# Scaled keys split over VectorE and ScalarE, and half of wo times the gradient on VectorE, in a decode layer's forward and backward pass

## The chip, the cores and the metric

The kernel runs on one core of a Trainium2 chip. A core has TensorE (matmuls, written PE in the profile; PEld is its weight loads), VectorE (DVE), ScalarE (ACT), GpSimd (POOL) and SyncE (SP), and 16 DMA engines that move data between HBM and the on-chip memory SBUF. Matmul results land in PSUM and are copied to SBUF by VectorE or ScalarE. Each engine runs its own instructions in order; between engines there are semaphores. The order of instructions on each engine and the waits are laid down by a scheduler when the kernel is built.

The metric is the device time of the kernel in microseconds (us), the median of several runs. Verdicts are taken at 2%.

## What is computed

One decoding step (one new token for each of two sequences) of a transformer layer, and its gradients. Attention reads the last W = 4096 of 32768 cached positions; 32 query heads share 8 heads of keys and values. Cut to what matters:

```python
def _A_ref(x, k_cache, v_cache, wq, wo):          # attention; Hq=32, Hkv=8, Dh=128, W=4096
    q = (x @ wq) ...                              # heads of the one new token
    k = k_cache[:, :, Sk - W:, :] ; v = v_cache[:, :, Sk - W:, :]   # each used by 4 query heads
    p = softmax(q . k * Dh ** -0.5)
    o = p . v
    return o.reshape(B, 1, Hq * Dh) @ wo
def _B_ref(x, w_gate, w_up, w_down):              # feed-forward, F=1792
    return (gelu(x @ w_gate) * (x @ w_up)) @ w_down
h  = x + _A_ref(layernorm(x), k_cache, v_cache, wq, wo)
h2 = h + _B_ref(layernorm(h), w_gate, w_up, w_down)
# outputs: h2, and the gradients for x, k_cache, v_cache, wq, wo, w_gate, w_up, w_down, given grad_out
```

The gradients of the two caches are as large as the caches, 2 x 8 x 32768 x 128 bf16 each, and zero outside the window: 235 MB of zeros are written.

## The kernel before

GpSimd issues 32 writes of zeros at the start, which run beside everything else. Then, for batch 0 and batch 1 in turn: `attention(b)`, `middle(b)` (output projection, feed-forward, and their backward pass down to the gradient of the attention output), `score_grads(b)`; then the weight gradients, and the stores of the gradients of K and V in the window.

Most of SBUF is one tile, `mem`, whose regions are reused by hand. The key buffers K_OFF[1] and the buffers PK_OFF[1] of batch 1 lie on the regions of w_down and of the small rows (OFF_R). `ef` are the exponentials of one group (4 heads, 4096 positions) in float32; `ee` is the same in bf16 with each value stored twice. In `attention`, for each group g and each unit u of 4 key columns:

```python
                KT_ps = ps_KT.tile([P, 8, P], BF16, tag="kt", name="KT_ps")
                for jj in range(8):
                    nc.tensor.transpose(out=KT_ps[:, jj, :], in_=Kt[b, g][:, u * 8 + jj, :], identity=ident_bf[:])
                KT = at(OFF_KT + (u % 2) * 2 * KIB, [P, 8, P], BF16, "KT")
                nc.scalar.copy(out=KT[:], in_=KT_ps[:])
                return KT
# ... (softmax of a group: maximum over all positions, then)
                ef = stA.tile([P, NJ, REP], F32, tag="ef", name="ef", bufs=1)
                ee = stA.tile([P, NJ, REP, 2], BF16, tag="ee", name="ee")
                nc.vector.tensor_tensor(out=ef[:], in0=S[:], in1=negm[:].unsqueeze(1).to_broadcast([P, NJ, REP]), op=ALU.add)
                nc.scalar.activation(out=ef[:], in_=ef[:], func=ACT.Exp)
                nc.vector.tensor_copy(out=ee[:], in_=ef[:].unsqueeze(3).to_broadcast([P, NJ, REP, 2]))
                Ef[g] = ee
                nc.vector.tensor_copy(out=eT[:].rearrange("p j a q -> p a j q")[:, :, :, g * REP:(g + 1) * REP],
                                      in_=ef[:].rearrange("p (a j) i -> p a j i", a=4))
                nc.vector.reduce_sum(out=lsum[:, 0, g * REP:(g + 1) * REP], in_=ef[:].rearrange("p j h -> p h j"), axis=AX.X)

            def m_unit(g, u, M_ps):
                pk = at(PK_OFF[b][u % n_pk], [P, pk_j, REP, DH], BF16, "pK")
                ef, Kb = Ef[g], Kt[b, g]
                j0 = u * pk_j
                shape = [P, pk_j, DH // 2, 2]
                for i in range(REP):
                    nc.vector.tensor_tensor(out=pk[:, :, i, :].rearrange("p j (d t) -> p j d t", t=2),
                                            in0=Kb[:, j0:j0 + pk_j, :].rearrange("p j (d t) -> p j d t", t=2),
                                            in1=ef[:, j0:j0 + pk_j, i, :].unsqueeze(2).to_broadcast(shape), op=ALU.mult)
                for a, src in enumerate((Vt[b, g], Kb)):
                    for jj in range(pk_j):
                        j = j0 + jj
                        c = j % 4
                        nc.tensor.matmul(out=oPK_ps[32 * c:32 * c + REP, a, :], lhsT=eT[:, j % 8, j // 8, g * REP:(g + 1) * REP],
                                         rhs=src[:, j, :], start=(j < 4 and a == 0), stop=(j >= NJ - 4), skip_group_check=True)
                for jj in range(pk_j):
                    j = j0 + jj
                    nc.tensor.matmul(out=M_ps[:], lhsT=Vt[b, g][:, j, :], rhs=pk[:, jj, :, :].rearrange("p i d -> p (i d)"),
                                     start=(j == 0), stop=(j == NJ - 1))

```

M is the sum over positions of v times the scaled keys; it is used later for the gradient of q. `finish(g)` copies oPK_ps and M_ps to SBUF (M on ScalarE). The loop over units makes the transposed keys and the scores of group g + 1 beside the units of group g:

```python
            softmax(0)
            for g in range(HKV):
                if g:
                    prefetch(b, g)
                M_ps = ps_M.tile([P, REP * DH], F32, tag="M", name="M_ps")
                more = g + 1 < HKV
                for u in range(n_u):
                    v, first = u // kt_every, u % kt_every == 0
                    if more and v < 4 and first:
                        nxt = kt_unit(g + 1, v)
                        if v:
                            s_unit(g + 1, v - 1, kts)
                        kts = nxt
                    m_unit(g, u, M_ps)
                    if more and v == 3 and u % kt_every == kt_every - 1:
                        s_unit(g + 1, 3, kts)
                        softmax(g + 1)
                finish(g, M_ps)
```

Loads of keys and values are issued by SyncE as buffers come free (`load_k`, `load_v` in `prefetch`); the values of group g lie at g * 8 KiB. At the end of attention the weights come back, and for batch 1 the two rows:

```python
K_OFF = ([OFF_WG + (g % 4) * 8 * KIB for g in range(HKV)],
         [OFF_WD, OFF_WD + 8 * KIB, 32 * KIB, 40 * KIB, 48 * KIB, 56 * KIB, OFF_WD, OFF_WD + 8 * KIB])
PK_J = 4
PK_OFF = ([OFF_WG + 32 * KIB + i * 4 * KIB for i in range(3)],
          [OFF_WD + 16 * KIB + i * 4 * KIB for i in range(2)])
# ...
    dh2_x = at(OFF_XR, [66, D], BF16, "xr")
    dh2_bf, x_32, dh_bf = dh2_x[0:B, :], dh2_x[32:32 + B, :], dh2_x[64:64 + B, :]

    def load_rows(eng):
        eng.dma_start(out=dh2_bf, in_=grad_out.rearrange("b s d -> (b s) d"))
        eng.dma_start(out=x_32, in_=A_x.rearrange("b s d -> (b s) d"))
# ... in prefetch(b, g), for b == 1:
        else:
            if g == 0:
                for i in range(4):
                    load_k(1, i)
                    load_v(1, i)
                load_k(1, 4)
                load_k(1, 5)
            elif g in (1, 2):
                load_k(1, g + 5)
            elif g - 3 + 4 < HKV:
                load_v(1, g + 1)
# ... for both:
        if g == HKV:
            if b == 0:
                load_wg_wu()
            load_wd()
            if b == 1:
                load_rows(nc.sync)
```

In `middle(b)`, the first matmuls, and the product of wo with the gradient dh, in which every 128 rows of wo are transposed by TensorE in four pieces, copied to SBUF, and multiplied:

```python
            attn_ps = ps_B.tile([B, D], F32)
            nc.tensor.matmul(out=attn_ps[:], lhsT=ident_bf[32:32 + B, 32:32 + B], rhs=x_32, start=True, stop=False)
# ...
            for r in range(NOR):
                nc.tensor.matmul(out=attn_ps[:], lhsT=O2[:, r, :], rhs=wo_sb[:, r, :], start=False, stop=(r == NOR - 1))
# ... feed-forward, forward and backward; for b == 1 ffn_ps with w_down
    def tblock(ps_pool, src_block):
        ps = ps_pool.tile([P, 4, P], BF16, tag="ps_tb", name="ps_tb")
        for a in range(4):
            nc.tensor.transpose(out=ps[:, a, :], in_=src_block(a), identity=ident_bf[:])
        dst = at(OFF_KT + (tb_i[0] % 3) * KIB, [P, 4, P], BF16, "tb")
        tb_i[0] += 1
        evac(dst[:], ps[:])
        return dst
# ...
            ln_bwd(d_ln2_ps[:].rearrange("b a p -> b p a"), ln2[:], rstd2, dh2_bf, f"2{b}", dh, at(OFF_R0, [B, D], F32, "tmp"))
            nc.vector.tensor_copy(out=dh_bf, in_=dh[:])
            dhT = transpose_rows(ps_B.tile([P, NDR, B], BF16, tag="sm", name="psT_dh"), dh_bf, f"dh{b}", strided=False, p0=64)

            dO2_ps = ps_B.tile([P, NOR, B], F32, tag="da", name="dO2_ps")

            def use_woT(r, woT):
                for nt in range(NDR):
                    nc.tensor.matmul(out=dO2_ps[:, r, :], lhsT=woT[:, nt, :], rhs=dhT[:, nt, :], start=(nt == 0), stop=(nt == NDR - 1))
            pipelined(NOR, lambda r: tblock(ps_W, lambda nt: wo_sb[:, r, nt * P:(nt + 1) * P]), use_woT, depth=2)
            # ... dO_sel, which reads dO2_ps[:, :, b]
```

`evac` copies from PSUM on VectorE and ScalarE in turn. `pipelined(n, produce, consume, depth)` runs produce `depth` items ahead.

## Time and profile before

| | |
|---|---|
| time, median of 3 runs | 809.6 us (809.58 to 809.68) |
| span of the profiled run | 807.8 us, mean granted TensorE clock 0.801 |
| busy: PE, PEld, DVE, ACT, POOL | 596.8, 325.7, 463.7, 283.1, 36.5 us |
| moved by DMA | 332.46 MB, mean 412 GB/s |
| of which zeros written by GpSimd's queue | 234.88 MB |

How to read it. A row of the page's groups has the line of the kernel, engine, operation, output and inputs with shapes, the count, then busy time in us and mean ns of one, then the engine's idle time just before and what ended it. The chain follows the work that ended last back to the start; in order of time each row has its start, its length, and what ran or what was waited for. In the page's strip the span is cut into 40 slices of about 20 us; a digit is a busy share in tenths. Where a line number is that of a helper (`evac`, `tblock`), the tile's name tells which use it is: ps_tb are the weight transposes of `middle`, KT_ps the transposed keys, VT_ps the transposed values of `score_grads`.

### The profile page before, as it was taken

The numbers are of one execution on the slowest core, as the hardware profiler recorded it, in microseconds if no ns is written. First come the engines' busy times: TensorE is split into PE (matmuls) and PEld (weight loads), VectorE is DVE, ScalarE is ACT, GpSimd is POOL, SyncE is SP. The second block draws the span as 40 slices with busy tenths as digits, with TensorE's granted clock in tenths as the row PEclk, the third lists the DMA queues.
The fourth block names the chain that finished last, engine by engine and source line by source line (L and its number), as shares of the span: only waits on it lengthen the run. The fifth ranks groups of instructions, "written<-read, shape, count | busy, mean of one in ns | idle before, by whom it ended". The sixth has DMA issues, their size and how long they took to land.

```text
span 807.8 us, 12954 instructions
## 1 busy us (share of the span) xinstructions
PE 596.8 (74%) x5350; PEld 325.7 (40%) x5350; DVE 463.7 (57%) x1133; ACT 283.1 (35%) x408; POOL 36.5 (5%) x51
## 2 busy tenths in 40 slices
PE   3998798469788729796767268778899596696681
PEld 3555454155576515453323135564443142232220
DVE  2798799023433218685666212536746628999991
ACT  1533220023334413241210103234644444586681
POOL 4100000000010000000000000000000000000000
PEclk9999999757759859998888666857955586889996
DMA  9999999999999999999999999999999999998887
GB/s 366 414 423 414 422 426 419 424 425 422 423 423 420 414 424 422 422 422 421 423 421 425 424 425 423 423 422 423 421 422 423 426 424 422 422 413 363 337 344 291
DMA packets 69467, 332.46 MB, mean 412 GB/s; under 512 B 1808, under 2 KB 1824, under 8 KB 59296
## 3 DMA queue, kind: packets, MB, share of 16 engines
q0 software_dynamic: 57856, 234.88, 87.3%
q1 hardware_dynamic: 11540, 96.75, 49.3%
q8 instruction: 42, 0.69, 0.3%
q10 hardware_dynamic: 12, 0.01, 0.1%
q14 instruction: 17, 0.14, 0.0%
HBM read 49.30 MB, written 282.33 MB: 411 GB/s over the span
## 4 chain that ended last, share of the span: by engine, by line
PE 41%; DMA 15%; DVE 14%; ACT 9%; issue 3%; ACTq 0%; SPq 0%; DVEq 0%
ACT mem L90 8%; PE ps_tb L231 7%; DMA mem<-in_A_v_cache_dram 7%; PE M_ps L393 5%; DVE mem L88 5%; PE ps_g L779 4%; PE VT_ps L600 4%; PE ps_gr L670 4%; PE dP_ps L609 4%; DMA mem<-in_B_w_down_dram 3%; DVE mem L382 3%; DMA mem<-in_A_k_cache_dram 3%; DMA mem<-in_A_x_dram 3%; PE d_ln_ps L538 2%; PE gu_ps L486 2%
## 5 line engine op out<-in xcount | busy, mean ns | idle before, releaser
L382 DVE TENSOR_TENSOR mem<-mem,ee 128x512 bf16<-128x512 bf16 x512 | 181.0, 421 | 39.1 <-PE M_ps L393 39.1
L393 PE MATMUL M_ps<-mem 128*128 128x512 bf16 x512 | 144.3, 402 | 11.3 <-DVE mem L382 8.8
L340 ACT COPY mem<-KT_ps 128x1024 bf16<-128x1024 bf16 x64 | 63.5, 1013 | 114.0 <-PE KT_ps L338 109.0
L231 PE MATMUL ps_tb<-ident_bf,mem 128*128 128x128 bf16 x664 | 82.7, 269 | 22.9 <-DMA mem<-in_B_w_down_dram 15.0
L779 PE MATMUL ps_g<-mem 128*128 128x512 bf16 x256 | 81.3, 416 | 24.5 <-ACT mem L90 21.3
L90 ACT COPY mem<-ps_tb 128x512 bf16<-128x512 bf16 x83 | 48.6, 586 | 116.3 <-PE ps_tb L231 67.2
L88 DVE COPY mem<-ps_tb 128x512 bf16<-128x512 bf16 x83 | 35.2, 424 | 91.7 <-PE ps_tb L231 62.2
L88 DVE CAST mem<-ps_g 128x512 bf16<-128x512 f32 x128 | 82.9, 688 | 7.3 <-PE ps_g L779 4.7
L90 ACT CAST mem<-ps_g 128x512 bf16<-128x512 f32 x128 | 75.0, 586 | 31.1 <-DVE mem L88 27.5
L231 PEld LDWEIGHTS <-mem 128*128 128x128 bf16 x664 | 56.0, 130 | 49.6 <-issue 29.3
L338 PE MATMUL KT_ps<-ident_bf,mem 128*128 128x128 bf16 x512 | 48.2, 244 | 25.8 <-DMA mem<-in_A_k_cache_dram 21.0
L393 PEld LDWEIGHTS <-mem 128*128 128x128 bf16 x512 | 44.1, 100 | 56.3 <-issue 22.9
L779 PEld LDWEIGHTS <-mem 128*128 128x128 bf16 x256 | 26.4, 103 | 78.6 <-issue 64.5
L104 POOL DMA_DIRECT2D out_dram<-zt x32 | 33.7, 1143 | 515.3 <-DMA out_dram<-zt 505.0
L338 PEld LDWEIGHTS <-mem 128*128 128x128 bf16 x512 | 36.8, 109 | 33.8 <-DMA mem<-in_A_k_cache_dram 21.8
L609 PE MATMUL dP_ps<-mem 128*128 128x512 bf16 x128 | 45.0, 437 | 4.8 <-ACT mem L90 4.8
L389 PE MATMUL oPK_ps<-mem 128*4 128x128 bf16 x1024 | 33.6, 236 | 19.9 <-DMA mem<-in_A_v_cache_dram 19.9
L600 PEld LDWEIGHTS <-mem 128*128 128x128 bf16 x512 | 37.1, 109 | 24.6 <-issue 17.2
L600 PE MATMUL VT_ps<-ident_bf,mem 128*128 128x128 bf16 x512 | 46.2, 241 | 0.9 <-DVE pkT L576 0.9
L90 ACT COPY mem<-VT_ps 128x1024 bf16<-128x1024 bf16 x33 | 34.0, 1031 | 33.9 <-PE VT_ps L600 25.6
L88 DVE CAST mem<-ps_gr 128x512 bf16<-128x512 f32 (+1 forms) x40 | 26.8, 671 | 28.8 <-PE ps_gr L670 28.7
L670 PE MATMUL ps_gr<-mem 2*128 2x512 bf16 (+1 forms) x78 | 32.9, 508 | 13.8 <-DVE mem L690 10.3
(247 smaller groups left out, 548.1 us busy)
## 6 DMA issues: line engine op xcount, KB each, us to landing
out_dram<-zt POOLq DMA_DIRECT2D x32, 7168.0 KB, 164.1
out_dram<-mem SPq DMA_DIRECT2D x36, 1024.0 KB, 16.6
mem<-in_A_k_cache_dram SPq DMA_DIRECT2D x16, 1024.0 KB, 13.9
mem<-in_A_v_cache_dram SPq DMA_DIRECT2D x16, 1024.0 KB, 27.2
out_dram<-mem SPq DMA_DIRECT2D x5, 1792.0 KB, 18.3
mem<-in_A_wq_dram SPq DMA_DIRECT2D x1, 4096.0 KB
mem<-in_A_wo_dram SPq DMA_DIRECT2D x1, 4096.0 KB
mem<-in_B_w_down_dram SPq DMA_DIRECT2D x2, 1792.0 KB, 25.4
```

Source lines behind the costliest of these rows:

```text
L88: nc.vector.tensor_copy(out=out, in_=in_)
L90: nc.scalar.copy(out=out, in_=in_)
L104: nc.gpsimd.dma_start(out=zero_regions[i].bitcast(F32).rearrange("(p k e) -> p k e", p=P, k=nper), in_=zt[:].unsqueeze(1).to_broadcast([P, ...
L231: nc.tensor.transpose(out=ps[:, a, :], in_=src_block(a), identity=ident_bf[:])
L338: nc.tensor.transpose(out=KT_ps[:, jj, :], in_=Kt[b, g][:, u * 8 + jj, :], identity=ident_bf[:])
L340: nc.scalar.copy(out=KT[:], in_=KT_ps[:])
L382: nc.vector.tensor_tensor(out=pk[:, :, i, :].rearrange("p j (d t) -> p j d t", t=2), in0=Kb[:, j0:j0 + pk_j, :].rearrange("p j (d t) -> p ...
L393: nc.tensor.matmul(out=M_ps[:], lhsT=Vt[b, g][:, j, :], rhs=pk[:, jj, :, :].rearrange("p i d -> p (i d)"), start=(j == 0), stop=(j == NJ - 1))
L600: nc.tensor.transpose(out=VT_ps[:, jj, :], in_=Vt[b, g][:, a * 8 + jj, :], identity=ident_bf[:])
L609: nc.tensor.matmul(out=dP_ps[:, c, :], lhsT=dOpad[:, w0:w0 + P], rhs=VT[:, c * 4:(c + 1) * 4, :].rearrange("d a k -> d (a k)"), start=(i = ...
L670: nc.tensor.matmul(out=ps[:, :n], lhsT=lhsT_fn(k), rhs=rhs_fn(k), start=True, stop=True)
L779: nc.tensor.matmul(out=ps[:, a2, :], lhsT=lhs_bf[:, jp * P:(jp + 1) * P], rhs=rhs_bd[:, ap * 2 + a2, gq * 4:(gq + 1) * 4, :].rearrange("q ...
```

## The change

Three parts:

- Scaled keys: instead of four VectorE products per unit with the doubled bf16 weights `ee`, VectorE makes 11 of the 16 blocks (4 key columns x 4 heads) in two products with the float32 weights `ef`, and ScalarE the other 5 as scaled copies. The doubled weights and their cast go. The transposed keys are copied by VectorE and ScalarE in turn, not by ScalarE alone. The matmuls into oPK_ps alternate between values and keys for each column.
- The rows of grad_out and x get a tile of their own (`rows`), so that batch 1 no longer loads them again; the row dh has its own place in the row region.
- wo times dh: TensorE transposes and multiplies 16 of the 32 row blocks, all copied by ScalarE; for the other 16 dh is broadcast to all partitions by one matmul, and VectorE multiplies each block of wo by it, with the sum along the row. The aim is to use VectorE, which has little to do there, beside TensorE.

```diff
+    rows = ctx.enter_context(tc.tile_pool(name="rows", bufs=1))
...
-    dh2_x = at(OFF_XR, [66, D], BF16, "xr")
-    dh2_bf, x_32, dh_bf = dh2_x[0:B, :], dh2_x[32:32 + B, :], dh2_x[64:64 + B, :]
-    def load_rows(eng):
-        eng.dma_start(out=dh2_bf, in_=grad_out.rearrange("b s d -> (b s) d"))
-        eng.dma_start(out=x_32, in_=A_x.rearrange("b s d -> (b s) d"))
-    def load_x(off):
-        x_bf = at(off, [B, D], BF16, "x")
+    dh2_x = rows.tile([34, D], BF16)
+    dh2_bf, x_32 = dh2_x[0:B, :], dh2_x[32:32 + B, :]
+    x_bf = at(OFF_X, [B, D], BF16, "x")
+
+    def load_x():
-        return x_bf
-    x_bf = load_x(OFF_X)
+    load_x()
-    load_rows(nc.scalar)
+    nc.scalar.dma_start(out=dh2_bf, in_=grad_out.rearrange("b s d -> (b s) d"))
+    nc.scalar.dma_start(out=x_32, in_=A_x.rearrange("b s d -> (b s) d"))
...
-    def tblock(ps_pool, src_block):
+    def tblock(ps_pool, src_block, on_act=False):
-        evac(dst[:], ps[:])
+        if on_act:
+            nc.scalar.copy(out=dst[:], in_=ps[:])
+        else:
+            evac(dst[:], ps[:])
...
-                load_rows(nc.sync)
+                load_x()

...
-                nc.scalar.copy(out=KT[:], in_=KT_ps[:])
+                evac(KT[:], KT_ps[:])
...
-                ef = stA.tile([P, NJ, REP], F32, tag="ef", name="ef", bufs=1)
-                ee = stA.tile([P, NJ, REP, 2], BF16, tag="ee", name="ee")
+                ef = stA.tile([P, NJ, REP], F32, tag="ef", name="ef")
-                nc.vector.tensor_copy(out=ee[:], in_=ef[:].unsqueeze(3).to_broadcast([P, NJ, REP, 2]))
-                Ef[g] = ee
+                Ef[g] = ef
...
                 pk = at(PK_OFF[b][u % n_pk], [P, pk_j, REP, DH], BF16, "pK")
                 ef, Kb = Ef[g], Kt[b, g]
                 j0 = u * pk_j
-                shape = [P, pk_j, DH // 2, 2]
-                for i in range(REP):
-                    nc.vector.tensor_tensor(out=pk[:, :, i, :].rearrange("p j (d t) -> p j d t", t=2),
-                                            in0=Kb[:, j0:j0 + pk_j, :].rearrange("p j (d t) -> p j d t", t=2),
-                                            in1=ef[:, j0:j0 + pk_j, i, :].unsqueeze(2).to_broadcast(shape), op=ALU.mult)
-                for a, src in enumerate((Vt[b, g], Kb)):
-                    for jj in range(pk_j):
-                        j = j0 + jj
-                        c = j % 4
-                        nc.tensor.matmul(out=oPK_ps[32 * c:32 * c + REP, a, :], lhsT=eT[:, j % 8, j // 8, g * REP:(g + 1) * REP],
-                                         rhs=src[:, j, :], start=(j < 4 and a == 0), stop=(j >= NJ - 4), skip_group_check=True)
+                for (n, h0, h1) in ((pk_j, 0, 2), (pk_j - 1, 2, 3)):
+                    shape = [P, n, h1 - h0, DH]
+                    nc.vector.tensor_tensor(out=pk[:, 0:n, h0:h1, :], in0=Kb[:, j0:j0 + n, :].unsqueeze(2).to_broadcast(shape),
+                                            in1=ef[:, j0:j0 + n, h0:h1].unsqueeze(3).to_broadcast(shape), op=ALU.mult)
+                for (jj, i) in [(jj, 3) for jj in range(pk_j)] + [(pk_j - 1, 2)]:
+                    nc.scalar.activation(out=pk[:, jj, i, :], in_=Kb[:, j0 + jj, :], func=ACT.Copy, scale=ef[:, j0 + jj, i:i + 1])
+                for jj in range(pk_j):
+                    j = j0 + jj
+                    c = j % 4
+                    e_j = eT[:, j % 8, j // 8, g * REP:(g + 1) * REP]
+                    nc.tensor.matmul(out=oPK_ps[32 * c:32 * c + REP, 0, :], lhsT=e_j, rhs=Vt[b, g][:, j, :],
+                                     start=(j < 4), stop=(j >= NJ - 4), skip_group_check=True)
+                    nc.tensor.matmul(out=oPK_ps[32 * c:32 * c + REP, 1, :], lhsT=e_j, rhs=Kb[:, j, :],
+                                     start=False, stop=(j >= NJ - 4), skip_group_check=True)
                 for jj in range(pk_j):
                     j = j0 + jj
                     nc.tensor.matmul(out=M_ps[:], lhsT=Vt[b, g][:, j, :], rhs=pk[:, jj, :, :].rearrange("p i d -> p (i d)"),
...
             pipelined(len(jobs), prod_w, use_w, depth=2)
 
             if b == 1:
-                ffn_ps = ps_B.tile([B, D], F32)
+                ffn_ps = ps_B.tile([B, D], F32, tag="tmp", name="ffn_ps")
-            nc.vector.tensor_copy(out=dh_bf, in_=dh[:])
-            dhT = transpose_rows(ps_B.tile([P, NDR, B], BF16, tag="sm", name="psT_dh"), dh_bf, f"dh{b}", strided=False, p0=64)
+            nc.vector.tensor_copy(out=dh_bf[:], in_=dh[:])
+            dhT = transpose_rows(ps_B.tile([P, NDR, B], BF16, tag="sm", name="psT_dh"), dh_bf[:], f"dh{b}", strided=False)
 
             dO2_ps = ps_B.tile([P, NOR, B], F32, tag="da", name="dO2_ps")
+            dO2 = small.tile([P, NOR], F32, name=f"dO2_{b}", tag="dO2")
+            NPE = 16
+            dhB_ps = ps_B.tile([P, D], F32, tag="gu", name="dhB_ps")
+            nc.tensor.matmul(out=dhB_ps[:], lhsT=ident_bf[0:B, b:b + 1].to_broadcast([B, P]), rhs=dh_bf[:], start=True, stop=True)
+            junk = ps_B.tile([P, D], F32, tag="tmp", name="junk")
+            for r in range(NPE, NOR):
+                nc.vector.scalar_tensor_tensor(out=junk[:], in0=wo_sb[:, r, :], scalar=1.0, in1=dhB_ps[:], op0=ALU.mult, op1=ALU.mult,
+                                               accum_out=dO2[:, r:r + 1])
 
             def use_woT(r, woT):
                 for nt in range(NDR):
                     nc.tensor.matmul(out=dO2_ps[:, r, :], lhsT=woT[:, nt, :], rhs=dhT[:, nt, :], start=(nt == 0), stop=(nt == NDR - 1))
-            pipelined(NOR, lambda r: tblock(ps_W, lambda nt: wo_sb[:, r, nt * P:(nt + 1) * P]), use_woT, depth=2)
+            pipelined(NPE, lambda r: tblock(ps_W, lambda nt: wo_sb[:, r, nt * P:(nt + 1) * P], on_act=True), use_woT, depth=2)
+            nc.scalar.copy(out=dO2[:, 0:NPE], in_=dO2_ps[:, 0:NPE, b])
             dO_sel = small.tile([P, 4, NOR], F32, name=f"dO_sel{b}", tag="l4")
-            nc.vector.tensor_tensor(out=dO_sel[:], in0=dO2_ps[:, :, b].unsqueeze(1).to_broadcast([P, 4, NOR]),
+            nc.vector.tensor_tensor(out=dO_sel[:], in0=dO2[:].unsqueeze(1).to_broadcast([P, 4, NOR]),
                                     in1=maskQ[:].unsqueeze(2).to_broadcast([P, 4, NOR]), op=ALU.mult)
             dOT_ps = ps_B.tile([P, HQ], F32, tag="sm", name="dOT_ps")
             nc.tensor.matmul(out=dOT_ps[:], lhsT=dO_sel[:].rearrange("p q r -> p (q r)"), rhs=selH[:], start=True, stop=True)
... (renamed offsets, selB and the reload of x for the last stage follow from this)
```

## The prediction

> **What bounds the kernel now.** I read the page first, then the chain in order of time, then busy time by stage, then single stretches of the timeline. The page says that the transfer engines are full nearly throughout:
>
> ```profile
> DMA  9999999999999999999999999999999999998887
> GB/s 366 414 423 414 422 426 419 424 425 422 423 423 420 414 424 422 422 422 421 423 421 425 424 425 423 423 422 423 421 422 423 426 424 422 422 413 363 337 344 291
> DMA packets 69467, 332.46 MB, mean 412 GB/s; under 512 B 1808, under 2 KB 1824, under 8 KB 59296
> ```
>
> 332.46 MB at the plateau of about 423 GB/s is 786 us: a floor near 790 with ramp and drain. The span is 807.8, so a faster chain of computation can give about 17 us and no more. The last three slices (337, 344, 291 GB/s) are not full: there the end is set by computation, and a later chain moves the end one for one. [...] The chain in order of time names them:
>
> ```profile
> 135.09 4.13 DVE mem L382 x12
> 139.27 1.02 PE M_ps L393 x4
> 140.32 25.43 DMA mem<-in_B_w_down_dram
> ...
> 275.25 23.32 DMA mem<-in_A_k_cache_dram
> ...
> 364.65 28.45 DMA mem<-in_A_v_cache_dram
> ...
> 406.92 25.95 DMA mem<-in_A_v_cache_dram
> ...
> 446.13 20.99 DMA mem<-in_A_x_dram
> 467.74 9.68 PE attn_ps L472 x32
> ```
>
> So the path is attention of batch 0, load of w_down, middle, score gradients, load of K, attention of batch 1 with two V loads in it, the reload of two rows, middle, weight gradients, stores. Busy time by stage (columns: stretch, length, then busy us and count of PE, PEld, DVE, ACT, POOL, granted clock, DMA share, GB/s) for the two attentions and the two stretches of wo times the gradient:
>
> ```profile
> 26.30:140.30 114.00, 102.16 (x1265) 57.55 (x1263) 101.12 (x325) 32.87 (x42) 3.14 (x3) 0.99 1.43 420
> 214.30:236.00 21.70, 17.93 (x238) 16.72 (x238) 6.46 (x17) 8.82 (x16) 1.04 (x1) 0.50 1.29 422
> 301.00:446.30 145.30, 113.26 (x1264) 59.94 (x1263) 102.57 (x328) 32.91 (x43) 7.30 (x7) 0.87 1.58 423
> 519.70:541.00 21.30, 17.46 (x238) 16.37 (x237) 6.22 (x15) 8.79 (x15) 1.04 (x1) 0.50 1.32 422
> ```
>
> VectorE is busy 101 of 114 us in attention 0 and ScalarE only 33: VectorE paces it. In the wo stretches TensorE is busy 18 of 21.7 and VectorE is nearly idle.
>
> [...] the paired product takes 421 ns for 512 elements, while a bf16 product with a weight broadcast along the innermost axis takes 1218 for 1024.
>
> ```profile
> L382 DVE TENSOR_TENSOR mem<-mem,ee 128x512 bf16<-128x512 bf16 x512 | 181.0, 421 | 39.1 <-PE M_ps L393 39.1
> L259 DVE TENSOR_TENSOR mem<-rows_7332,maskB 128x1024 bf16<-128x1024 bf16 x4 | 4.6, 1218 | 0.0
> L88 DVE COPY mem<-VT_ps 128x1024 bf16<-128x1024 bf16 x31 | 21.4, 691 | 27.8 <-PE VT_ps L600 27.2
> L340 ACT COPY mem<-KT_ps 128x1024 bf16<-128x1024 bf16 x64 | 63.5, 1013 | 114.0 <-PE KT_ps L338 109.0
> ```
>
> [...] The trace agrees on the slope (copies of 512 and 1024 elements take 586 and 1013, 0.834 ns per element)[...]. [...] the 2 KB row of A_x issued at 446.13 lands 21 us later, behind the 1.8 MB of w_down issued at 442.5.
>
> **The change, part by part.**
>
> *Scaled keys (both attentions).* Per unit of four key columns before: 4 products at a cadence of 0.34 us (16 of them take 5.46 us at 26.31), 1.37. After: one product of 1024 and one of 384 elements with a float32 weight[...]. From the 1.135 cadence of the L259 rows (three take 3.49) I estimate 1.13 and 0.465, 1.60 together. ScalarE takes the other 5 of 16 key blocks: 128 elements extrapolate to 266 ns from the copies[...]. KT evacuation goes half to VectorE (about 0.62 in sequence, 2 per group). Per group of 8 units, VectorE: 12.8 + 1.25 + 1.8 for the softmax chain (2.0 now, less the pair cast) = 15.85, where now it is 11.0 + 2.0 = 13.0. That 13.0 fits the trace: the last three M copies of attention 0 are 13.05 (a full group) and 11.1 (the last, without softmax) apart. ScalarE: 11.7 + 2.0 + 0.6 + 0.3 = 14.6. Three in-order engines within 15% of each other will stall each other. With three pk buffers in attention 0 I take 16.7 per group. With two in attention 1 I take 18.0, because a unit with a KT copy on ScalarE (1.45 + 1.0) can't be hidden behind 1.6.
>
> Attention 0: 7 x 16.7 + 13.5 + 3 of load waits (now about 10 of the 114 us are excess; slower groups hide most of it) = 133.4 against 114.0: **+19.5**.
>
> Attention 1 has the V loads in its chain. V of group g+2's buffer is the K of group g, so from the start s: group 3 ends at s+72, V5 is issued 1 before and lands 28 later, s+99; group 5 ends s+117; V7 lands s+142; the last group ends s+156. Now it is s+144.3. **+12**.
>
> *wo times the gradient.* Before: 32 blocks of 4 transposes, copy, 4 matmuls at 0.63 us each (214.3 to 234.7). After: 16 blocks, all copied by ScalarE, about 0.7 each and three ready before, some 10 us; beside them 16 VectorE products with sums of 512 elements, one input and the output in PSUM. The nearest row is the 745 ns of the score product, with a cadence of about 0.66, plus 0.07 for reading the accumulator: 0.73 x 16 = 11.7, starting at 214.9 after one matmul of broadcast. Ready at 226.6, not 234.7: **-8 in each middle**, -16.
>
> *Rows kept in a tile of their own.* The gradient and x rows are no longer overwritten by pk and need no reload. TensorE waits for it now:
>
> ```profile
> 467.16 0.58 PE L464 MATMUL attn_ps<-mem,ident_bf 2*2 2x512 bf16 x1 [16.77 <-DMA mem<-in_A_x_dram]
> ```
>
> In batch 0 the same matmul starts 0.9 us after the last M copy (141.2 against 140.3). It would be ready near 448, so **-19**. Some 17 of the 20 transposes that were done in the wait now come after attn_ps, **+1**. w_down itself is needed first by ffn_ps, 23.5 us after attn_ps now; landing 21 after the end of attention, it is just in time.
>
> *Unchanged:* the load of w_down before middle 0 (25.4) and of K before attention 1 (23.3): the same buffers, released by the same work. The order of transfers is the same but for the two rows. *oPK:* now two matmuls per column group in a row, not four groups in turn; 1024 of them are busy 33.6 us. [...]
>
> Sum: +19.5 + 12 - 16 - 19 + 1 = -2.5 on the span. I put the median at **809.0**, because my stall allowance is more likely too small than too large.
>
> **The rivals.** (1) *Attention alone decides.* ScalarE at 14.6 and VectorE at 15.85 chase each other through two pk buffers, and groups take 18.5 and 20. Then it is +34 and +24 against -34: about 832. For it: in attention 1 the groups take 16.4 already, where VectorE needs 13. Against: there TensorE is granted 0.87 and stalls[...]. (2) *The gains come and attention hides its loss*, since loads end last in attention 1: +15, +6, -35, so 795. The floor of transfers (about 790) then begins to bind. (3) *The wait for the rows is only renamed*: ffn_ps waits for w_down instead, which would give back up to 3 us by my times, or 10 if the load is slower: 812 to 819. (4) *The VectorE products outlast TensorE's half*, at 1.0 us each from PSUM on both sides: 16 us and -4 per middle, 817.
>
> **Range and chances.** The two attention terms are uncertain by 8 us each, the wo term by 3, the wait by 3. Rooted together this is about 12, capped below by the floor. The range that should hold it 8 times in 10 is 794 to 827. Two per cent are 16.2 us: faster 0.07, same 0.83, slower 0.10.
>
> **What would show it.** VectorE's key products at 1.13 and 0.46 cadence, ScalarE's at 0.29; groups of 16.7 and 18 between M copies; attention 0 ending near 160; the wo stretches 12 us long; no transfer of A_x in the chain; the first attn_ps matmul of batch 1 within 3 us of the last M copy. I am wrong if groups take over 18.5, if the products with sums take 1 us, or if ffn_ps waits long for w_down.

## The result and the profile after

The changed kernel takes 814.05 us (median; 813.82 to 814.53) against 809.59 for the kernel before (809.39 to 809.68) beside it: a ratio of 1.0056, 95% interval 1.0039 to 1.0074. The prediction was 809, range 794 to 827. Within 2%, as said; but the two are different by more than the measurement is uncertain, and the experiments show that the steps which happened to cancel were not all the right ones. In the experiments single executions were disturbed at times (rows_only's lay between 836 and 857); the ratios leave these out and the medians don't, so the two need not agree.

The page of the changed kernel, its strip of transfers and three of its groups (the columns are those of the page before):

```profile
DMA  8999999999999999999999999999999999986968
GB/s 364 414 425 415 421 423 422 428 419 424 421 423 423 416 417 425 423 421 422 422 422 422 424 423 424 423 423 423 428 417 423 425 425 425 410 364 283 390 284 343
...
L377 DVE TENSOR_TENSOR mem<-mem,ef 128x1024 bf16<-128x1024 bf16 (+1 forms) x256 | 213.6, 876 | 13.7 <-PE M_ps L391 13.6
L380 ACT ACTIVATE mem<-mem,ef 128x128 bf16<-128x128 bf16 x640 | 201.3, 391 | 22.6 <-PE M_ps L391 19.6
L391 PE MATMUL M_ps<-mem 128*128 128x512 bf16 x512 | 144.1, 403 | 32.9 <-DVE mem L377 30.4
```

The last five slices are not full: computing sets the end. The new products stand where the old ones stood (L382 before: 181.0 us), and TensorE's M products now wait 30.4 us for them instead of 8.8.

The same stretches as before, in busy time by stage (stretch, length, then busy us and count of PE, PEld, DVE, ACT, POOL, granted clock, DMA share, GB/s): attention 0, the wo product of middle 0, attention 1, the wo product of middle 1.

```profile
26.30:159.20 132.90, 107.70 (x1259) 58.25 (x1256) 122.69 (x203) 115.30 (x348) 4.97 (x5) 0.96 1.46 421
232.20:245.00 12.80, 7.54 (x109) 7.02 (x108) 12.12 (x33) 7.42 (x14) 1.04 (x1) 0.52 1.29 422
318.50:477.00 158.50, 113.56 (x1265) 59.36 (x1263) 124.60 (x206) 117.37 (x350) 7.95 (x8) 0.87 1.59 422
533.10:552.90 19.80, 9.49 (x113) 7.69 (x113) 17.08 (x40) 8.01 (x15) 2.04 (x2) 0.50 1.37 423
```

Attention 0 is longer by 19, VectorE and ScalarE both nearly full. From the first dO matmul to dO_sel (the start of each, in the table below) the wo product fell from 20.4 to 12.7 us in middle 0, and in middle 1 only from 21.0 to 19.8: that is the first surprise. The chain in order of time shows the loads that it waits for from the second half of attention 1 on:

```profile
387.86 29.18 DMA mem<-in_A_v_cache_dram
...
431.81 30.29 DMA mem<-in_A_v_cache_dram
...
472.72 33.65 DMA mem<-in_B_w_down_dram
```

The reload of x is gone from it, and w_down has taken its place.

From both traces, the times (us) at which each stage was reached, each the start of what is named unless an end or a landing is; the differences are taken before rounding. "Last dP" is the last matmul pair of score_grads(0), "first VT" is the first transpose of score_grads(1), "last ps_gr" the end of the last weight-gradient matmul that is made beside it; after that come wq's gradients, the dK and dV products and the stores.

```
                            before   after   behind by
last M copy, attention 0     140.3   159.2     18.9
first dO matmul, middle 0    214.3   232.2     17.9
last dP, score_grads(0)      274.6   285.5     10.9
K for attention 1 landed     298.6   316.1     17.5
last M copy, attention 1     446.3   476.9     30.7
first dO matmul, middle 1    519.7   533.1     13.4
dO_sel, middle 1             540.7   552.9     12.2
first VT                     548.9   557.9      9.1
last ps_gr                   641.3   649.6      8.2
end of the span              807.8   812.4      4.6
```

### The profile page after: what moved, and what is told of

The parts are those of the page before. It is cut to its first block, busy times and chain, and to the rows that moved or that the text cites. A ratio compares the mean times of both kernels' runs of the same rounds, so it can differ in the third digit from the quotient of the medians.

```text
span 812.4 us, 12842 instructions
## 1 busy us (share of the span) xinstructions
PE 584.4 (72%) x5096; PEld 309.1 (38%) x5096; DVE 519.7 (64%) x925; ACT 444.0 (55%) x1018; POOL 35.9 (4%) x49
## 4 chain that ended last, share of the span: by engine, by line
PE 25%; DVE 12%; DMA 11%; ACT 5%; issue 1%; ACTq 0%; DVEq 0%; SPq 0%
DMA mem<-in_A_v_cache_dram 7%; DVE mem L88 4%; PE ps_g L786 4%; DMA mem<-in_B_w_down_dram 4%; PE ps_gr L677 4%; ACT mem L90 3%; PE ps_tb L225 3%; PE VT_ps L608 3%; PE dP_ps L617 2%; DVE mem L377 2%; PE M_ps L391 2%; DVE mem L256 2%; PE ps_gq L757 1%; PE d_ln_ps L734 1%; DVE mem L697 1%
## 5 line engine op out<-in xcount | busy, mean ns | idle before, releaser
L377 DVE TENSOR_TENSOR mem<-mem,ef 128x1024 bf16<-128x1024 bf16 (+1 forms) x256 | 213.6, 876 | 13.7 <-PE M_ps L391 13.6
L380 ACT ACTIVATE mem<-mem,ef 128x128 bf16<-128x128 bf16 x640 | 201.3, 391 | 22.6 <-PE M_ps L391 19.6
L391 PE MATMUL M_ps<-mem 128*128 128x512 bf16 x512 | 144.1, 403 | 32.9 <-DVE mem L377 30.4
L786 PE MATMUL ps_g<-mem 128*128 128x512 bf16 x256 | 80.8, 414 | 24.8 <-ACT mem L90 23.3
L391 PEld LDWEIGHTS <-mem 128*128 128x128 bf16 x512 | 43.2, 101 | 98.5 <-DVE mem L377 54.4
L225 PE MATMUL ps_tb<-ident_bf,mem 128*128 128x128 bf16 x536 | 64.3, 258 | 22.2 <-DMA mem<-in_B_w_down_dram 14.2
L90 ACT COPY mem<-ps_tb 128x512 bf16<-128x512 bf16 x51 | 29.8, 585 | 92.0 <-PE ps_tb L225 49.1
L90 ACT COPY mem<-KT_ps 128x1024 bf16<-128x1024 bf16 x32 | 32.1, 1002 | 64.6 <-PE KT_ps L335 64.6
L88 DVE COPY mem<-ps_tb 128x512 bf16<-128x512 bf16 x51 | 21.6, 424 | 65.9 <-PE ps_tb L225 57.3
L225 PEld LDWEIGHTS <-mem 128*128 128x128 bf16 x536 | 43.2, 129 | 47.4 <-issue 31.1
L786 PEld LDWEIGHTS <-mem 128*128 128x128 bf16 x256 | 26.2, 103 | 78.5 <-issue 64.3
L335 PEld LDWEIGHTS <-mem 128*128 128x128 bf16 x512 | 37.4, 111 | 46.5 <-DMA mem<-in_A_k_cache_dram 27.5
L90 ACT COPY mem<-VT_ps 128x1024 bf16<-128x1024 bf16 x33 | 34.0, 1031 | 31.9 <-PE VT_ps L608 30.7
L608 PEld LDWEIGHTS <-mem 128*128 128x128 bf16 x512 | 38.2, 110 | 24.2 <-issue 16.6
L385 PE MATMUL oPK_ps<-mem 128*4 128x128 bf16 x512 | 28.6, 232 | 23.0 <-DMA mem<-in_A_v_cache_dram 22.5
L88 DVE CAST mem<-ps_gr 128x512 bf16<-128x512 f32 (+1 forms) x40 | 26.6, 670 | 27.8 <-PE ps_gr L677 27.7
```

The source lines that it names most:

```text
L88: nc.vector.tensor_copy(out=out, in_=in_)
L90: nc.scalar.copy(out=out, in_=in_)
L377: nc.vector.tensor_tensor(out=pk[:, 0:n, h0:h1, :], in0=Kb[:, j0:j0 + n, :].unsqueeze(2).to_broadcast(shape), in1=ef[:, j0:j0 + n, h0:h1]. ...
L380: nc.scalar.activation(out=pk[:, jj, i, :], in_=Kb[:, j0 + jj, :], func=ACT.Copy, scale=ef[:, j0 + jj, i:i + 1])
L608: nc.tensor.transpose(out=VT_ps[:, jj, :], in_=Vt[b, g][:, a * 8 + jj, :], identity=ident_bf[:])
L786: nc.tensor.matmul(out=ps[:, a2, :], lhsT=lhs_bf[:, jp * P:(jp + 1) * P], rhs=rhs_bd[:, ap * 2 + a2, gq * 4:(gq + 1) * 4, :].rearrange("q ...
```

## The experiments

All twelve, in the order in which they were made. A chaser is a small load that is issued right behind a lone one; where the order is held, TensorE may not begin the sums of a group ahead of the last M product of the group before it. "last ps_gr" is read from the run's trace as above.

```
run            what it is                                        us     ratio (95%)             last ps_gr
rows_only      before + rows kept                              845.76   1.0348 (1.0323-1.0374)    673.5
keys_only      before + new key split                          842.73   1.0408 (1.0370-1.0445)    679.8
no_keys        changed kernel, old keys                        833.26   1.0295 (1.0276-1.0313)    667.5
no_wo          changed kernel, wo all on TensorE               821.43   1.0147 (1.0131-1.0163)    655.9
rows_held      rows_only, TensorE's order held                 809.64   1.0016 (0.9985-1.0047)    631.0
no_keys_held   no_keys, TensorE's order held                   808.62   0.9984 (0.9962-1.0006)    626.9
after_late_o   changed kernel, o_bhd behind the products       812.62   1.0012 (0.9976-1.0048)    650.1
after_chase    changed kernel + chasers (in a shared buffer)   948.53   1.1683 (1.1594-1.1773)    782.2
nk_chase       no_keys_held + chasers, ef in its pool          810.84   1.0004 (0.9978-1.0029)    563.7
nk_split       nk_chase, 8 stores as 120 + 8 rows              813.22   1.0039 (1.0024-1.0053)    565.3
after_chase2   changed kernel + chasers                        812.44   1.0035 (1.0023-1.0048)    592.0
nk_seven       nk_chase, 3 stores as 119 + 9 rows              819.86   1.0128 (1.0112-1.0143)    562.2
```

Read the last column against the profiled span of each run: in the changed kernel, keys_only, rows_only, no_keys, no_wo and after_late_o the end comes 162.7 to 164.2 us after the last ps_gr (812.4 - 649.6 = 162.8; 844.0 - 679.8 = 164.2; 837.4 - 673.5 = 163.9), and 164.6 us in after_chase. That is what the rest of the computing takes. In rows_held, no_keys_held, nk_chase and after_chase2 the last ps_gr comes 10 to 78 us earlier than in the kernel before, and the span ends between 806.8 and 810.7 all the same. Something else is waiting there.

### One part at a time: rows_only, keys_only, no_keys, no_wo

My theory was that each part moves the chain by what it is worth. The rival was that what is gained comes back as another wait.

rows_only puts the rows tile into the kernel before. For want of 0.5 KiB the float32 weights had to go somewhere else:

```diff
-    dh2_x = at(OFF_XR, [66, D], BF16, "xr")
+    dh2_x = rows.tile([34, D], BF16)                 # no reload before middle 1
-                ef = stA.tile([P, NJ, REP], F32, tag="ef", name="ef", bufs=1)
+                ef = at(OFF_R + 9 * KIB, [P, NJ, REP], F32, "ef")
```

> The kernel before with the rows of x and of the output gradient kept in a tile of their own, and nothing else (the float32 softmax weights lie in the main tile for lack of room). Theory A, the parts add up along the chain: the wait of 16.8 us before the second middle goes, the w_down load (issued at the last M copy, landed 24.6 us later in the kernel before, wanted by ffn_ps about 24.5 us after it) is just in time, and some 2 us come back at the end: 793 to 796 us. Theory B, the wait is only renamed: ffn_ps waits for w_down as it does in the changed kernel (5 us or more), and the gain is half or less: 801 to 806 us.

keys_only is the kernel before with the new kt_unit, softmax and m_unit lines of the change. no_keys is the changed kernel with the old ones (and ef placed as in rows_only). no_wo is the changed kernel with all 32 blocks of wo on TensorE:

```diff
-            pipelined(NPE, lambda r: tblock(..., on_act=True), use_woT, depth=2)
+            pipelined(NOR, lambda r: tblock(...), use_woT, depth=2)    # no dhB_ps, no products with sums
```

> The kernel before with the new split of the scaled keys (VectorE and ScalarE, float32 weights) and nothing else. Theory A, the parts add up: +19 us in the first attention, +7 us in the wait for the K load before the second, +13 us in the second, some 3 us given back at the end: 843 to 848 us. Theory B, slower attention only fills time in which loads were waited for: +20 to +26 us, 830 to 836 us.

> The changed kernel with the scaled keys as they were before (all on VectorE, pairs): rows kept and half of the wo product on VectorE. Theory A: rows -14 to -16, wo -7.7 in the first middle and -1 in the second, where VectorE's queue holds other work between the products: 784 to 789 us. Theory B, the end is set by the transfers (332 MB, some 790 us at the rate seen) and what is gained before is waited for at the end: 794 to 800 us.

> The changed kernel with the whole wo product on TensorE again: rows kept and the new key split. Theory A, the wo half is worth what the first middle shows (-7.7) and about -1 in the second: 822 to 824 us. Theory B, it is worth -8 in both, and something else cost the second middle its gain: 828 to 831 us. Theory C, a wait for a load that follows hides it: 814 to 817 us.

keys_only came at 842.73, just under theory A's 843 to 848: the split on its own costs 33 us, and the wait for the x row is still in it. no_wo came at 821.43: wo is worth 7.4 us in all, which is theory A's -7.7 in one middle and about nothing in the other, not the -16 of my prediction.

rows_only and no_keys fit neither theory: to *remove* a wait, and a wait and a slow product, cost 28 and 24 us by the ratios. The group and the chain of rows_only, attention 1 to w_down, show where:

```profile
L386 PE MATMUL oPK_ps<-mem 128*4 128x128 bf16 x1024 | 34.9, 238 | 76.5 <-DMA mem<-in_A_v_cache_dram 73.2
```

```profile
350.20 28.29 DMA mem<-in_A_v_cache_dram
...
383.42 27.24 DMA mem<-in_A_v_cache_dram
...
415.59 31.51 DMA mem<-in_A_v_cache_dram
...
452.01 31.36 DMA mem<-in_A_v_cache_dram
```

All four late V loads are in the chain, one after the other, where the kernel before has two (364.65 and 406.92). Up to the last M copy of attention 0 the two traces are the same to 0.1 us (140.3). What differs is the order of TensorE's instructions. In the kernel before, no sum of values or keys (oPK_ps) of a group stands ahead of the last M product of the group before it. In rows_only, in attention 1 alone, 43 to 49 of the next group's 64 do, for six groups in a row. TensorE works its queue in order, so it stops at the first sum that needs V of the next group (73.2 us of waiting for V in the group above), with M products of this group ready behind it; this group doesn't finish, its K buffer isn't free, and the next V load, which goes into that buffer, isn't issued. Each load's latency is then paid in full. The scheduler chose that order when the program was built; all that I had given it was a tile for the rows and another place for the 512 bytes a row of ef. Which of the two moved the sums was not tried one by one; the trace of the changed kernel, which has the tile for the rows and ef in its pool (and the new key split), has no sum ahead.

### The order held: rows_held, no_keys_held

```diff
+                    last_M[0] = nc.tensor.matmul(out=M_ps[:], ...)      # and prev_M = last_M at the end of a group
+                        with tc.issue_after(prev_M[0].ins):             # on TensorE, not ahead of that product
                             nc.tensor.matmul(out=oPK_ps[...], ...)
```

> rows_only with one thing more: on TensorE the value and key sums of a group may not stand ahead of the last M product of the group before it (as they stand in the kernel before). Theory A: rows_only was slow because its TensorE queue held 43 to 49 of the 64 sums of the next group ahead of the end of this group, so that each lone V load was waited for in full; with the order held, the second attention takes some 147 us again instead of 198, and the row wait of 16.8 us is saved: 793 to 797 us. Theory B, the order is innocent and keeping the rows slows the loads themselves: 830 to 846 us as in rows_only. Theory C, order explains the loss, but ffn_ps then waits for w_down: 799 to 804 us.

> no_keys with the order of TensorE's queue held in the same way. Theory A, the parts add up along the chain: 784 to 789 us. Theory B, the transfers set the end (332 MB, some 790 us at the rate seen): 792 to 800 us. Theory C, order is innocent: 832 us again.

Order explains the loss: with nothing else changed the profiled span falls from 837.4 to 808.0, and attention 1 (K landed to last M copy) takes 158 us instead of 198. It still isn't the 148 of the kernel before; ef shares bytes with a pK buffer in these two runs. The traces point to that for some 5 of the 10 us: from the landing of K to the first M copy, rows_held takes 24.8 us, the kernel before 19.6, and nk_chase (below), with ef back in its pool, 19.8. The rest was not tried.

But neither came to 793 or 784. Rows kept: the first dO matmul of middle 1 stands at 511.2, 8.5 us ahead of the kernel before, and the last ps_gr 10.3 us ahead. Then the gain is gone: 809.64. With wo as well the last ps_gr is 14.4 us ahead: 808.62. The page of rows_held:

```profile
DMA  9999999999999999999999999999999999999992
GB/s 365 413 423 413 422 424 422 424 424 422 423 423 420 418 421 422 421 422 422 424 423 423 424 422 423 423 423 423 419 426 425 426 422 418 423 418 423 393 409 106
```

The transfers now are full, or nearly so, to the last slice but one, and the last slice is nearly empty (106). The landings of the last stores show why; each 1 MB store counts up its semaphore 16 times:

```
last store of     issued   15 of 16 landed by   16th landed   lag
before            793.12          803.45            806.40     3.0
after             800.79          810.34            810.86     0.5
rows_held         786.97          793.96            806.45    12.5
```

I read this as one of the 16 DMA engines being behind; the trace names no engine, but in the kernel before the last 8 packets of the last store (8 KB, 0.309 us each) run singly from 803.50 to 805.95, one every 0.305 us. It is behind earlier in the kernel before and in the changed kernel too: stores of theirs, issued at 742.74 and 722.78, have lags of 12.5 and 12.4 us. There the computing at the end leaves it time to catch up; once the stores come earlier, it sets the end.

### VectorE's queue in middle 1: after_late_o

The changed kernel's wo product in middle 1 as VectorE's part of the timeline has it (start, us, engine, line, operation, out and in):

```profile
540.05 0.14 DVE L559 DVE_READ_ACCUMULATOR junk<-mem,dhB_ps 128x1 f32 x1
542.57 0.22 DVE L651 COPY o_bhd<-o_ps 64x128 bf16<-64x128 bf16 x1 [2.38 <-PE o_ps L650]
542.71 0.68 DVE L559 SCALAR_TENSOR_TENSOR junk<-mem,dhB_ps 128x512 f32<-128x512 bf16 x1
543.31 0.13 DVE L559 DVE_READ_ACCUMULATOR junk<-mem,dhB_ps 128x1 f32 x1
543.31 1.21 DVE L645 TENSOR_TENSOR mem<-o_bhd,maskC 64x1024 bf16<-64x1024 bf16 x1
544.45 0.68 DVE L559 SCALAR_TENSOR_TENSOR junk<-mem,dhB_ps 128x512 f32<-128x512 bf16 x1
...
552.88 0.28 DVE L568 TENSOR_TENSOR dO_sel_6210<-dO_1_6029,maskQ 128x128 f32<-128x128 f32 x1
```

TensorE is done with its half at 542.2. VectorE, which should be done at 545.7, first waits 2.38 us for a transpose that stands behind TensorE's half, and then alternates with the four products of build_R (L645, 1.21 each). Neither has to do with wo; they belong to the weight gradients, which come later in the program. after_late_o gives o_bhd a buffer that is free only behind dO_sel:

```diff
-    o_bhd = small.tile([NBH, DH], BF16, tag="bhd")
+    o_l4 = small.tile([P, 4, HQ], F32, name="o_l4", tag="l4")      # the buffer of dO_sel and prod4
+    o_bhd = o_l4[0:NBH].rearrange("p a q -> p (a q)").bitcast(BF16)[:, 0:DH]
```

> The changed kernel with o_bhd in a buffer that comes free only after dO_sel and the product behind it, so that its copy and the four build_R products stand behind the 16 products with sums in VectorE's queue. Theory A, the second middle lost its gain to these instructions between the products: the stretch from the first dO matmul to dO_sel takes 12 to 13 us instead of 19.8, of which some 3 go to build_R, which is then on the chain: 809 to 811 us. Theory B, the stretch is short but all of it is waited for later: 813 to 815 us.

The stretch fell from 19.8 to 15.4 us (533.5 to 548.9). The rest, against the 12.7 of middle 0, is one more line of that run's timeline, again from the weight gradients:

```profile
543.48 0.68 DVE L656 CAST mem<-DH_ps 64x512 bf16<-64x512 f32 x1 [2.15 <-ACT dO L566]
```

But the chain of that run then goes through build_R from 552.75 to 557.5, and the last ps_gr is at 650.1 against 649.6. The median of 812.62 lies between what the two theories said, and the interval of its ratio (0.9976 to 1.0048) overlaps that of the changed kernel: inconclusive as a gain. The order cost the stretch some 4 us or more, and none of this is seen to reach the end.

### A lone load and its semaphore: after_chase

In attention 1 the trace shows three phases of a lone 1 MB load. V load of the kernel before, issued at 364.65: its 128 packets of 8 KB move between 372 and 379.5; then come the 4-byte packets that count up the semaphore, and most of these take 9 to 15 us each; landed at 393.11. In a train of loads (V and K loads issued every 4.4 us or so from 242.5 to 273.5) the same packets take 0.2 us, and each load lands 13 to 16 us after its issue, but the last of the train (K, issued at 275.25) needs 23.3. Ahead of the fill, whose first packet moves at 18.5 us, the 4 MB of wq and the first 1 MB of K, issued at 1.2 and 1.7, landed after 12.1 and 14.2 us. Why these packets take 9 to 15 us for the lone load and 0.2 us in a train, with the same fill of about 424 GB/s beside both, is not in the trace. So I tried whether a small load behind a lone one on the same ring (SyncE's queue), a chaser, lets it through:

```diff
+    def chaser():
+        dst = at(OFF_R + 9 * KIB + (ch_i[0] % 2) * 512, [P, 2 * DH], BF16, "chase")
+        nc.sync.dma_start(out=dst[:], in_=Kv[:, 0, 0, 0:2, :].rearrange("p j d -> p (j d)"))
                 load_v(1, g + 1)
+                chaser()                    # likewise behind lone K loads and w_down; TensorE's order held
```

> The changed kernel with a small load of 512 B a row (into a free corner) issued behind every lone load: K loads of the first attention, the last six K and V loads and w_down in the second, w_down in the first; TensorE's order held. In the trace a lone 1 MB load has its data in some 15 us after its issue, and then its 4-byte semaphore packets take 4 to 12 us; in a train of loads they take 0.2 us. Theory A, a packet of the same ring behind them lets them through: the lone loads land 7 to 10 us earlier, K before the second attention -8, two V waits -8 each, w_down -6 to -8 twice: 785 to 798 us. Theory B, the packets wait for the fill's writes whatever follows: 812 to 816 us.

948.53, and yet half of theory A was right. The K load issued at 336.46 landed at 352.83, 16.4 us later, and the next three lone loads took 15.9 to 16.5, where the changed kernel shows 27 to 30. It is the chaser, now the last on the ring, that takes 28 to 32 us. And something waited for it:

```profile
337.44 32.24 DMA mem<-in_A_k_cache_dram
369.68 0.02 issue
369.70 1.24 DVE mem L394
```

L394 is a scaled-keys product. The corner that I took for free, OFF_R + 9 KiB, lies in the pK buffers of attention 1 (OFF_WD + 16 KiB and on, 8 KiB): the next product had to wait until the chaser had written there, in every group. It is the same corner in which ef stands in rows_only and no_keys.

### Chasers without the collision: nk_chase and after_chase2

Buffers used only near the end of the program (bhd, rowsb, dup) went to that corner instead, ef went back to its pool, and the chasers got four buffers of 32 bytes a row of their own.

```diff
+    ch_t = [small.tile([P, 16], BF16, name=f"chase{i}") for i in range(4)]
+        with tc.issue_after(last_ld[0].ins):
+            nc.sync.dma_start(out=ch_t[ch_i[0] % 4][:], in_=Kv[:, 0, 0, 0, 0:16])
```

> Rows kept, half of wo on VectorE, scaled keys as before, TensorE's order held, the small end-only buffers moved so that nothing shares room with the scaled keys, and behind each lone load a chaser: a load of 32 bytes a row into buffers of its own. Theory A, two things at once: lone K, V and w_down loads land some 16 us after their issue instead of 26 to 31 (as the loads of after_chase did, whose chasers' buffer the scaled keys had to wait for), so the second attention takes 115 to 128 us instead of 147 and the start of the weight gradients comes 35 to 60 us earlier; but the end stays, because the DMA engine that is last (12.4 us behind the others on the last store of rows_held) has no less to do: 804 to 808 us. Theory B, the chain of computing sets the end and the transfers follow it: 760 to 785 us. Theory C, chasers do nothing without the collision: 808 us and a second attention of 140 us or more.

> The changed kernel with chasers behind its lone loads as in nk_chase (buffers of their own), TensorE's order held and the small end-only buffers moved; the new key split stays. Theory A: with the load waits gone the slower scaled keys no longer reach the end: the second attention takes about 130 us instead of 161, the weight gradients start 55 to 75 us earlier, and the time is that of the transfers, 806 to 811 us, as for the old keys. Theory B, the key split costs at the end even then: 813 us or more.

Theory A in both: 810.84 and 812.44 (the first 2.8 above, the second 1.4 above its range). Lone K and V loads of attention 1 landed 15.3 to 16.6 us after their issue and w_down after 17.7. A follower of two rows doesn't do this: in the changed kernel x's two-row load is issued 4.0 us behind w_down on the same ring, and w_down took 33.65. A chaser has 128 rows. In the trace of the kernel before, a load of 128 rows counts up its semaphore 16 times and a two-row transfer twice; whether that is the difference was not tried. The chain of nk_chase still names two V loads, with little of a wait left in them:

```profile
323.46 16.50 DMA mem<-in_A_v_cache_dram
...
370.21 16.62 DMA mem<-in_A_v_cache_dram
```

Attention 1 (first to last M copy) took 105.5 us instead of 128.1 in the kernel before; the last ps_gr came at 563.7, 77.6 us earlier. The page of nk_chase:

```profile
DVE  2797988124732397878623857467379999920000
...
DMA  8999999999999999999999999999999999999993
GB/s 365 413 414 421 418 428 420 420 423 422 423 419 416 420 423 417 421 420 421 422 422 423 423 423 424 420 424 425 423 423 421 420 417 415 417 417 417 421 422 101
```

VectorE has nothing left to do from about 730 us on; the fill of zeros goes on to 806.4, and the program ends there. This settles what bounds the kernels whose computing is early: 332 MB of transfers end at some 807 to 811, however early it is. In the last 10 us of the fill the trace has only 65 packets of 4 KB, one every 0.154 us. By my estimate that is one engine again: 4 KB in 0.154 us are 26.6 GB/s, and a sixteenth of the plateau of 423 is 26.4. With the new key split (after_chase2) the computing is 28 us later than with the old (592.0 against 563.7), and it makes 1.6 us.

### Which engine is last: nk_split and nk_seven

If one engine is late, give it less. To which engines a transfer is dealt is in no profile, and no run before these two showed it; what the expectations assume of it is my estimate. In theory A of each, the split takes packets off the late engine, in theory B it doesn't.

```diff
-                        nc.sync.dma_start(out=dst_v[:, b, gq * 4 + a * 2 + b2, :, :], in_=sts[a][:, b2, :, :])
+                        n_store[0] += 1
+                        for p0, p1 in ((0, 120), (120, P)) if n_store[0] in range(5, 13) else ((0, P),):
+                            nc.sync.dma_start(out=dst_v[p0:p1, b, gq * 4 + a * 2 + b2, :, :], in_=sts[a][p0:p1, b2, :, :])
```

nk_seven has 119 in place of 120, and range(5, 8).

> nk_chase with 8 of the 32 last 1 MB stores issued as 120 rows and 8 rows. [...] Theory A, the last engine is the one left out[...]: each split store takes 8 packets of 8 KB, 2.5 us, off it, and its lag of some 12 us is gone: 795 to 800 us. Theory B, the last engine is another: it gets one packet more per split store at most, and the time stays: 805 to 811 us. Theory C, the end isn't set by one engine: no change against nk_chase.

> nk_chase with 3 of the last stores issued as 119 rows and 9 rows. [...] In nk_split the end came 2.4 to 2.6 us later, which is the 8 extra packets of 0.31 us[...]. Theory A, [...] it does 21 packets of 8 KB less, 6.5 us, the others up to 30 more, and the end comes some 3 to 6 us earlier than in nk_chase: 804 to 808 us. Theory B, [...] 30 packets more, 9 us: 817 to 821 us.

Theory B twice. Beside one increment at the issue, the pieces of a split store show 15 and 8 increments in nk_split, 7 and 9 in nk_seven. If each increment stands for one engine and the rows are dealt evenly, which is an estimate from these counts and the 16 of a whole store, then an engine that has a share of both pieces gets 8 + 1 packets of a store in nk_split and 17 + 1 in nk_seven, where it had 8: 8 more over the 8 stores, and 30 more over the 3. At 0.31 us a packet that is 2.5 and 9.3 us; the runs took 2.4 (813.22 - 810.84) and 9.0 (819.86 - 810.84) longer. So the late engine has, by this estimate, a share of both pieces both times, and neither split relieved it. Which of the 16 it is was not shown. That the end came 2.4 and 9.0 us later is measured, that a single engine sets it is read from this, and why that engine is late isn't shown. One idea was that it also carries the packets of the queue that the page calls instruction (q8: 42 packets of 16 KB, 0.88 to 1.08 us each, none overlapping another). But in the kernel before, while zeros are written by one packet at a time (736 to 742), one of these packets runs from 738.96 to 739.90, and the zeros go on at their pitch of 0.47 us through it. So that packet at least didn't hold up the zeros, and the cause stays open.

No version beats the kernel before by more than the measurement is uncertain; no_keys_held, at 0.9984 (0.9962 to 1.0006), comes nearest.

## Why the prediction was right, and where it was not

The predicted time was 5 us too low and in range. By its own steps:

**"A floor near 790 ... a faster chain of computation can give about 17 us and no more": wrong, and it is the step that matters most.** 332.46 MB by the plateau rate takes the 16 engines as one. The last increment of a store lands up to 12.5 us after the other 15, and nk_chase puts the end at 808.8 with the computing 77 us ahead. The kernel before, at 807.8, was already on that floor and at the end of its computing at once. So rival 2 (795) could not have happened, and the most that any version won is some 1 us (no_keys_held), no more than the measurement is uncertain.

**"The last three slices are not full: there the end is set by computation, and a later chain moves the end one for one": right in kind.** The computing after the last ps_gr takes 163 to 165 us in all seven runs that are late. The kernel before needs 166.5, 3.7 more than the changed one: the late engine's lag on the last store (2.95 against 0.52) is 2.4 of that, and the rest I can't assign. Therefore a lateness of 8.2 at the last ps_gr became 4.6 at the end.

**Scaled keys, attention 0, +19.5: right**, +18.9. VectorE's products showed the predicted cadence (1.13 and 0.46). ScalarE's scaled copy takes 391 ns alone, 125 more than the 266 extrapolated from the copies, but five in a row take 1.57 us, 0.29 to 0.32 each; 0.29 was predicted. That 0.29, and with it the 1.45 a unit and the 14.6 a group, was my estimate: no trace of the kernel before has a scaled copy.

**Attention 1, +12: right sum, wrong terms.** From the landing of K to the last M copy it is 160.8 against 147.7, +13.1. But four of the groups take 15.9 to 16.8 us and not 18.0 (another takes 19.3); two pK buffers were enough for them. The V loads took 27 to 30 us where 28 and 26 were assumed, and the two groups that waited for one took 27, where in the kernel before three took 20.

**"Unchanged: ... K before attention 1": wrong.** The wait from the last dP pair of score_grads(0) grew from 24.0 to 30.7. I had taken a load's time as a property of the load. This one is the last of its train, and the same load took 23.3 us in the kernel before, 30.0 in the changed one, 22.0 in rows_only, and 15.2 in nk_chase with a chaser behind it. Why it varies between the first three wasn't found.

**Rows kept, -19 and +1: right in size; w_down "just in time": wrong.** x's matmul follows the last M copy after 0.85 us, where it waited to 467.16 before. But w_down took 33.65 us to land and ffn_ps waited for it:

```profile
PE ffn_ps L544 <- DMA mem<-in_B_w_down_dram: 7.7, 1, 7.7
```

The activations were ready at 501.43 and the products began at 506.41, so 5.0 of the 7.7 are its own: rival 3, at the size that it was given (3 to 10). From last M copy to first dO matmul the two kernels take 73.5 and 56.2 us, -17.3: 20.0 gained at attn_ps, 5.0 lost at ffn_ps, and 2.3 gained between that I can't assign.

**wo, -8 in each middle: right in middle 0 (-7.7), wrong in middle 1 (-1.2).** The product with its sum takes 0.69 us and its read 0.14, and the pair comes every 0.787 us, not 0.73; rival 4's 1.0 didn't come. In middle 1 the step "16 VectorE products" took their place in VectorE's queue for granted. The order was there to be read in the program's list of instructions: o_bhd, build_R and the DH copy stand between them. As build_R is then done, 3.1 us of it come back before the first VT (12.2 behind, then 9.1).

**The sum, -2.5: +8.2 at the last ps_gr.** The difference of 10.7 is the wait for K (6.7) and the second wo product (6.8), less build_R (3.1); the remaining steps come out within 1 us in sum. The median that I raised to 809 for longer stalls in attention was near for a reason that did not occur.

**Rival 1 (groups of 18.5 and 20, 832) fell**: groups took 16. The clock that was held against it, 0.87 granted to TensorE in attention 1, was the same in both kernels. What it feared was true in another way. The split alone makes 842.73, and the other two parts bring this to 814.05, 29 us, as long as computing sets the end.

## What to carry to other kernels

Before counting what a faster chain may bring, ask when the *last* DMA engine can be done, not what all bytes take at the mean rate: look whether the last store's sixteenth increment trails the fifteenth (by 12.5 us in rows_held). Where a program's own scheduler lays out the queues, compare the orders on each engine before comparing times, because a new tile and a moved buffer of 512 bytes a row can put a waiting instruction ahead of ready ones (some 28 us here), and hold the order where a load's latency depends on it. And a buffer shared by hand between two stages is free only if nothing in *either* stage writes it.

## What was not expected of the hardware

- A lone 1 MB load beside the fill of zeros lands 22 to 32 us after its issue; with a load of 128 rows of 32 bytes behind it on the same ring it lands after 15 to 17, and a two-row load behind it did not do that. The chaser itself then takes 23 to 35 us. Why a follower shortens the load before it wasn't found.
- The last of the 16 increments of a 1 MB store landed 12.5 us after the other 15 (rows_held). Splits of stores moved the end of the program by 2.4 and 9.0 us, 0.30 us for each of the 8 and 30 packets of 8 KB that they added, by the estimate above, to the engine behind it.
